# Loading order and step order in the head of a fused LayerNorm, state-space scan and gated-unit kernel

## The chip, the cores and the metric

The kernel runs on one core of a Trainium2 chip (trn2). The metric is the device time of one execution in microseconds (us). The kernel before was timed in three runs; their median is 185.26 us.

## The reference, cut to what matters

`x` has 2048 tokens of 448 features. Everything is computed from its normalised rows `xn`.

```python
xn = _layernorm(x)                        # 2048 x 448, no scale, no shift
s  = _A_ref(xn, Lambda_re, ..., Dskip)    # diagonal complex state-space scan over the tokens
g  = _silu(_B_ref(xn, w_gate, w_up, w_down))
return x + s * g

def _B_ref(x, w_gate, w_up, w_down):      # w_gate, w_up: 448 x 1792, w_down: 1792 x 448
    g = x @ w_gate
    u = x @ w_up
    return (_sigmoid(g) * u) @ w_down
```

## The kernel before, in words

The tokens are cut into 4 chunks (`c`) of 512, and each chunk into 4 tiles of 128 rows (`t` counts tiles from 0 to 15). A chunk needs the transposed rows `xnT`. It then passes through 14 steps that fill `hF` (7 "g" steps with `w_gate`, 7 "u" steps with `w_up`), a phase B (input matrix of the scan), the scan itself on VectorE, `down` (with `w_down`) and `yout` (output matrix of the scan, sum and store).

**A step.** The 448 features are contracted in 7 slices of 64 rows. `gu_mm` (lines 699 to 712) issues 7 pairs of matmuls per step: one of a pair (line 707) uses the lower 64 rows of TensorE and yields 128 columns of the first 896 of `w_gate` or `w_up`, the other (line 708) uses the upper 64 rows and yields 128 columns of the last 896. So the weight tiles `wG` and `wU` hold the lower half of the columns on partitions 0 to 63 and the upper half on 64 to 127, and step `m` of 7 needs its 128 columns of both halves. The two results fill the two banks of one of three PSUM slots, `gu[0]` to `gu[2]`, which the steps use in turn. `gu_evac` (lines 716 to 726) empties a slot: a g step by a tanh on ScalarE (line 721), a u step by one VectorE instruction (line 724). Two more banks, `acc[0]` and `acc[1]`, serve transposes, the phase B and the output.

**Order.** `Plan` (lines 74 to 242) records every operation with an engine, a planned cost and its dependences. It settles one order per engine from planned times, and the instructions are issued in that order. TensorE keeps the order in which the code adds its operations; VectorE does so too while `pl.seq` is true (lines 964 to 985); each DMA queue keeps the order of its loads. The `rate` of a load and its `slot` only enter the planned times. An engine works its list strictly in order, so an instruction that waits holds back all that follow it on its engine. The loads of SP and ACT share eight landing counters in turn: a load that reuses a counter is not issued before the earlier load on it has landed.

**The head, chunk 0.** For each of tiles 0 to 3: `stats` (VectorE, lines 424 and 425), `chain` (square root on ScalarE line 450, a copy of the mean on GpSimd line 451, reciprocal on VectorE line 452), `norm` (VectorE, line 469), `pe_transpose` (eight small TensorE instructions, lines 501 to 503, into `acc[0]` or `acc[1]`) and a copy to `xnT[0]` (tile 0 by ScalarE, line 506; the others by VectorE, line 509). TensorE first runs 11 warm-up matmuls on zeros (line 418). `columns` (lines 535 to 563) turns the three parameter rows `log_dt`, `Lambda_im`, `Lambda_re` (loaded by GpSimd's queue into `hF`) into columns with five small matmuls (lines 540 and 542) in `gu[2]`, copies them to `pv` by VectorE (line 546), and starts a chain of small GpSimd operations. From these ScalarE and VectorE make the tables of sines and cosines (`tables`, lines 570 to 605) that the scan needs.

TensorE's order in the head before is: warm-up; transposes of tiles 0 and 1; `columns`; g steps 0 and 1, each for tile 0 and then each for tile 1; transposes of tiles 2 and 3; g step 2 for tiles 0 and 1; g steps 0, 1, 2 for tiles 2 and 3 together; g steps 3 to 6 and u steps 0 to 6 for all four tiles; phase B.

The loads of the head before, in the order of their queues (sizes as the profile counts them):

- SP: x tile 0 (112 KB); lower half of w_gate for steps 0-1 (224 KB), 2-3 (224 KB) and 4-6 (336 KB); w_up steps 0-2, lower then upper half (336 KB each); x tiles 4 to 7 (448 KB); w_up steps 3-6, lower then upper half (448 KB each); D (`dbc`); then the transposing loads of B (`bT`, line 375) and the transposes of the normalised tiles 4 to 7.
- ACT: x tile 1 (112 KB); x tiles 2 and 3 (224 KB); upper half of w_gate for steps 0-1, 2-3 and 4-6.

Tiles 4 to 7 are the next chunk: `stats_for(1)` and `prepare(1)` normalise them (ScalarE, line 474), and DMA transposes write them to `xnT[1]`.

Of the kernel before, what the change touches and what calls it, by code (L numbers as in the profile page):

```python
# [14 lines left out]
ACT = mybir.ActivationFunctionType  # L15
# [5 lines left out]
P = 128  # L21
H = 64
# [4 lines left out]
TPC = L // P  # L27
# [35 lines left out]
def act(n, ap=0):  # L63
    return 0.05 + 0.000833 * n + 0.093 * ap
# [181 lines left out]
def kernel(  # L246
# [18 lines left out]
    V, A, G, T, Q = nc.vector, nc.scalar, nc.gpsimd, nc.tensor, nc.sync  # L265
# [80 lines left out]
    pl = Plan(185.0)  # L346
# [9 lines left out]
    def load_x(t0, n, q="SP", r=(), rate=230e3):  # L356
        load(q, [("x", t) for t in range(t0, t0 + n)], n * P * D * 2,
             x_all[:, t0:t0 + n, :], x_src[:, t0:t0 + n, :], r=r, rate=rate)

    BLK = {"g": [(0, 2), (2, 4), (4, 7)], "u": [(0, 3), (3, 7)]}  # L360

    def load_w(eng, k, half, b, r=(), rate=105e3):
        m0, m1 = BLK[k][b]
        ps = slice(half * H, half * H + H)
        c0 = half * 896
        load(eng, [("w", k, half, m) for m in range(m0, m1)], H * 7 * (m1 - m0) * P * 2,
             wgt[k][ps, :, m0 * P:m1 * P],
             wsrc[k][:, c0 + m0 * P:c0 + m1 * P].rearrange("(s p) f -> p s f", p=H), cost=0.65, r=r, rate=rate)

    def load_wd(h):  # L370
        fs = slice(h * 7, h * 7 + 7)
# [11 lines left out]
    def load_p(eng, k, r=()):  # L383
        load(eng, ("vrow", k), D * 2, vrow[k:k + 1, :], (A_log_dt, A_Lambda_im, A_Lambda_re)[k].unsqueeze(0), cost=0.75, r=r)
    load_x(0, 1, "SP")
    load_w("SP", "g", 0, 0, rate=90e3)
    load_w("SP", "g", 0, 1)
    load_x(1, 1, "ACT")
    load_x(2, 2, "ACT")
    load_w("ACT", "g", 1, 0, rate=90e3)  # L390
    load_w("SP", "g", 0, 2)
    load_w("ACT", "g", 1, 1)
    load_w("ACT", "g", 1, 2)
    load_p("POOL", 0)
    load_p("POOL", 1)
    load_p("POOL", 2)
# [7 lines left out]
    add("POOL", 0.1, lambda: G.memset(pio2[:], PI / 2), w=["pio2"])  # L404
    add("POOL", 0.6, lambda: G.iota(iota[:, 0:NTAB], pattern=[[1, NTAB]], base=0, channel_multiplier=0,
                                    allow_small_or_imprecise_dtypes=True), w=[("wv", 0)])
    for h in range(2):
        load_w("SP", "u", h, 0, rate=215e3)
    load_x(4, 4, rate=140e3)
    for h in range(2):  # L410
        load_w("SP", "u", h, 1, rate=260e3)
    load("SP", "dbc", P * D * 2, dbc[:], A_Dskip.unsqueeze(0).to_broadcast((P, D)))


# [6 lines left out]

    def stats(t):
        b = t % 3
        add("DVE", 0.6, lambda: V.bn_stats(out=bst[b][:], in_=x_all[:, t, :]), r=[("x", t)], w=[("bst", b)])  # L424
        add("DVE", 0.16, lambda: V.bn_aggr(out=mv[:, t, :], in_=bst[b][:]), r=[("bst", b)], w=[("mv", t)])

    def act_stats(t0):
# [67 lines left out]
    def pe_transpose(t):  # L495
        b, a, js = t % NXN, next_acc(), slice(t * P, t * P + P)
        tp = flat(acc[a][:].bitcast(BF16)[:, 0:7 * P], 7, P)

        def f():
            for s in range(6):  # L500
                T.transpose(tp[:, s, :], xn[b][:, s * H:s * H + P], ident[:, :])  # L501
            T.transpose(tp[0:H, 6, :], xn[b][:, 384:448], ident[:, :])
            T.transpose(tp[H:P, 6, :], xn[b][:, 0:H], ident[:, :])
        add("PE", 0.46, f, r=[("xn", b), "ident"], w=[("acc", a)])
        if t == 0:
            add("ACT", 0.85, lambda: A.copy(out=xnT[0][:, :, js], in_=tp[:, :, :]),
                r=[("acc", a)], w=[("xnT", 0, t, "a"), ("xnT", 0, t, "b")])
        else:
            add("DVE", 0.64, lambda: V.tensor_copy(out=xnT[0][:, :, js], in_=tp[:, :, :]),
                r=[("acc", a)], w=[("xnT", 0, t, "a"), ("xnT", 0, t, "b")])  # L510
# [9 lines left out]
    def xr(c, lo=0, hi=TPC):  # L520
        return [("xnT", c % 3, j, h) for j in range(lo, hi) for h in "ab"]
# [11 lines left out]


    def columns(a):
        vps = flat(gu[a][:, 0, 0:12], 4, 3)

        def f():
            for i in range(3):
                T.matmul(vps[:, i, :], lhsT=vrow[:, i * P:(i + 1) * P], rhs=ident[0:3, 0:3], start=True, stop=True)  # L540
            for h in range(2):
                T.matmul(vps[h * H:h * H + H, 3, :], lhsT=vrow[:, 384:448], rhs=ident[0:3, 0:3], start=True, stop=True)
        add("PE", 0.4, f, r=["ident"] + [("vrow", k) for k in range(3)], w=[("gu", a)])
        pv = sbt("pv", [3, 4], FP32)
        dt_b = C("dt", 4, BF16)
        add("DVE", 0.1, lambda: V.tensor_copy(out=pv[:].rearrange("p k i -> p i k"), in_=vps[:]), r=[("gu", a)], w=["pv"])
        dt_b = C("dt", 4, BF16)
        lim, lre = pv[:, 1, :], pv[:, 2, :]
        K.update(lre=lre, lim=lim)
        eb = expc[:].to_broadcast((P, 4))  # L550

        def small(fn, r, w):
            add("POOL", 0.4, fn, r=r, w=w)
        tt = lambda o, x, y, op: (lambda: G.tensor_tensor(out=o, in0=x, in1=y, op=op))
        theta, arg, turn, r_col = C("theta"), C("arg"), C("turn"), C("r")
# [9 lines left out]
    K = {}  # L565

    def silu_table():
        add("ACT", 1.3, lambda: A.preload_act_table_set("silu_and_others"), r=[("sd", t) for t in range(4)], w=["silutab"])

    def tables():  # L570
        turn = C("turn")
# [126 lines left out]

    def gu_mm(c, k, m, a, lo, hi, first):
        x = xnT[c % 3]  # L700
        ts = slice(lo * P, hi * P)
        w_ = wgt[k]
        ms = slice(m * P, m * P + P)

        def f():
            for s in range(7):
                T.matmul(gu[a][:, 0, ts], lhsT=w_[0:H, s, ms], rhs=x[0:H, s, ts], start=(s == 0), stop=(s == 6))  # L707
                T.matmul(gu[a][:, 1, ts], lhsT=w_[H:P, (s + 1) % 7, ms], rhs=x[H:P, s, ts],  # L708
                         start=(s == 0), stop=(s == 6))
        n = (hi - lo) * P  # L710
        return add("PE", 7 * (0.0028 + n / 2400.0) + (2 * SW if first else 0), f,
                   r=xr(c, lo, hi) + [("w", k, 0, m), ("w", k, 1, m)], w=[("gu", a)], name=f"{k}{c}.{m}")

    sg_n = [0]

    def gu_evac(c, k, m, a):
        b = m % NSIG
        th, tk = (hF[1][:, m, :, :], ("hF", 1, m)) if c == 0 else (sig[b][:], ("sig", b))
        ho, hk = hF[c % 2][:, m, :, :], ("hF", c % 2, m)
        if k == "g":  # L720
            add("ACT", act(1024), lambda: A.activation(th, gu[a][:], ACT.Tanh, scale=0.5),  # L721
                r=[("gu", a)], w=[tk])
        else:
            add("DVE", dve1(1024), lambda: V.scalar_tensor_tensor(out=ho, in0=th, scalar=1.0, in1=gu[a][:],  # L724
                                                                 op0=ALU.add, op1=ALU.mult),
                r=[("gu", a), tk], w=[hk])

    def gu_step(c, i, first=False):
        m, k = (i // 2, "gu"[i % 2]) if c else (i % 7, "gu"[i // 7])
# [237 lines left out]
    for t in (0, 1):  # L967
        chain(t, 1)
        norm(t)
    stats(2)  # L970
    stats(3)
    slots0 = [next_gu() for _ in range(3)]
    pe_transpose(0)
    pe_transpose(1)
    columns(slots0[2])
    for t in (2, 3):
        chain(t, 1)
        norm(t)
    for j in range(2):
        for m in range(2):  # L980
            gu_mm(0, "g", m, slots0[m], j, j + 1, not (j or m))
    pe_transpose(2)
    pe_transpose(3)
    silu_table()
    pl.seq = False
    gu_mm(0, "g", 2, slots0[2], 0, 2, True)
    for m in range(3):
        gu_mm(0, "g", m, slots0[m], 2, 4, False)
        gu_evac(0, "g", m, slots0[m])
    b_load()  # L990
    def stats_for(c):
        for t in range(4 * c, 4 * c + 4):
            if c not in (3,):
                stats(t)
            elif t % 2:
                act_stats(t - 1)
            if t % 2:
                chain(t - 1, 2)
# [96 lines left out]
```

## Time and profile before

| | |
|---|---|
| Time, three runs | 185.00, 185.26, 186.19 us; median 185.26 |
| Profiled execution, span on the core | 183.7 us |
| Lowest run minus span | 1.3 us |
| Median minus span | 1.6 us |
| TensorE busy | 177.4 us, 1402 matmuls |
| VectorE busy | 166.4 us, 296 instructions |
| ScalarE, GpSimd busy | 94.8 us, 34.2 us |
| Chain that ended last | TensorE 93%, DMA 3%, all else 4% |

The profile is of one execution. It gives its span from the first to the last instruction, and no device time of its own; what lies around the span is taken from the three runs. Times inside it count from the span's start. A line of the timeline has the start in us, the duration in us, the engine, the line of the code, the operation, what it writes and reads, and in brackets the time that the engine had stood idle with what ended the wait. "PEld" is the loading of weights into TensorE, and an engine with a "q" behind it is its instruction queue, where loads are issued.

### The profile page before, as it was taken

What the parts mean: (1) busy time and instruction counts of PE and PEld (TensorE: products, weight loads), DVE (VectorE), ACT (ScalarE), POOL (GpSimd) and SP (SyncE); (2) the same over time, 40 slices, a digit from 0 to 9 for tenths busy, and PEclk for the clock granted to TensorE, in tenths of its full rate; (3) what the DMA queues carried; (4) which work ended last, traced back from release to release, by engine and by line L of the source; (5) the groups of instructions that cost most, each with busy time, mean ns of one, the idle gap of its engine ahead of it and who ended that gap; (6) DMA issues with size and microseconds to landing.
All of it is one profiled execution on the core that took longest, in us unless ns stands there. A gap on an engine that the chain in (4) does not pass through costs nothing.

```text
span 183.7 us, 3601 instructions
## 1 busy us (share of the span) xinstructions
PE 177.4 (97%) x1402; PEld 90.4 (49%) x1402; DVE 166.4 (91%) x296; ACT 94.8 (52%) x152; POOL 34.2 (19%) x95
## 2 busy tenths in 40 slices
PE   7699999999999999999999999999999999999992
PEld 2585555465554444455554444444555444455551
DVE  3873899899999998999999999999999998999973
ACT  3689993958599978665310452367120445211100
POOL 7370465000048557700000000000000000000000
PEclk9999999999999999999999999999999999999999
DMA  5999994489801370243000000002000000001121
GB/s 137 255 225 223 155 166 90 90 256 266 231 0 26 74 82 21 50 82 71 0 2 0 29 0 0 4 0 75 0 4 0 25 25 5 25 0 52 57 73 50
DMA packets 30258, 13.44 MB, mean 73 GB/s; under 512 B 19744, under 2 KB 30240, under 8 KB 30240
## 3 DMA queue, kind: packets, MB, share of 16 engines
q1 hardware_dynamic: 28336, 12.05, 30.7%
q10 hardware_dynamic: 1808, 1.15, 2.5%
q8 instruction: 11, 0.18, 0.4%
q14 instruction: 7, 0.06, 0.1%
q0 software_dynamic: 96, 0.00, 0.0%
HBM read 6.77 MB, written 1.84 MB: 47 GB/s over the span
## 4 chain that ended last, share of the span: by engine, by line
PE 93%; DMA 3%; DVE 1%; issue 1%; POOL 1%; DVEq 0%; POOLq 0%
PE gu L707 45%; PE gu L903 14%; PE acc L932 11%; PE acc L903 9%; PE gu L775 8%; DMA hF<-in_A_Lambda_re_dram 3%; PE gu L708 2%; PE acc L778 2%; PE gu L761 2%; POOL hF L353 1%; PE acc L501 0%; DVE o_t L948 0%; PE acc L764 0%; DVE o_t L944 0%; DVE o_t L941 0%
## 5 line engine op out<-in xcount | busy, mean ns | idle before, releaser
L708 PE MATMUL gu<-xnT,wG 64*128 64x512 bf16 (+2 forms) x245 | 46.0, 333 | 0.0
L707 PE MATMUL gu<-xnT,wG 64*128 64x512 bf16 (+2 forms) x245 | 46.0, 333 | 0.0
L707 PE MATMUL gu<-xnT,wU 64*128 64x512 bf16 x196 | 45.8, 376 | 0.0
L708 PE MATMUL gu<-xnT,wU 64*128 64x512 bf16 x196 | 45.8, 376 | 0.0
L721 ACT ACTIVATE sig<-gu 128x1024 f32<-128x1024 f32 x21 | 21.3, 1021 | 22.0 <-PE gu L708 21.9
L903 PEld LDWEIGHTS <-hF 128*128 128x128 bf16 x224 | 21.9, 98 | 20.7 <-issue 0.2
L707 PEld LDWEIGHTS <-wG 64*128 64x128 bf16 x245 | 21.9, 94 | 18.7
L707 PEld LDWEIGHTS <-wU 64*128 64x128 bf16 x196 | 18.4, 94 | 22.1
L724 DVE SCALAR_TENSOR_TENSOR hF<-sig,gu 128x1024 bf16<-128x1024 f32 x21 | 25.5, 1216 | 2.9 <-PE gu L708 1.6
L903 PE MATMUL gu<-wd,hF 128*128 128x448 bf16 x140 | 27.9, 352 | 0.0
L842 DVE TENSOR_TENSOR_SCAN wv<-c_r,st,z 128x512 bf16<-128x512 f32 x18 | 22.9, 1276 | 0.0
L932 PE MATMUL acc<-cT,hT 128*128 128x448 bf16 (+1 forms) x112 | 22.6, 346 | 0.0
L708 PEld LDWEIGHTS <-wG 64*128 64x128 bf16 x245 | 21.8, 94 | 0.0
L909 ACT ACTIVATE g_t<-gu 128x448 bf16<-128x448 f32 x10 | 5.4, 541 | 29.2 <-DVE o_t L946 12.9
L708 PEld LDWEIGHTS <-wU 64*128 64x128 bf16 x196 | 18.4, 94 | 0.0
L789 ACT CAST bus<-gu 128x1024 bf16<-128x1024 f32 x12 | 11.9, 1011 | 12.4 <-PE gu L761 12.2
L903 PE MATMUL acc<-wd,hF 128*128 128x448 bf16 x84 | 16.9, 352 | 0.0
L775 PE MATMUL gu<-xnT,bT 128*128 128x512 bf16 x72 | 16.7, 379 | 0.0
L932 PEld LDWEIGHTS <-hT 128*128 128x128 bf16 x119 | 11.5, 98 | 10.1 <-issue 0.4
L424 DVE BATCH_NORM_STATS2 bst<-x_all 128x6 f32<-128x448 bf16 x12 | 7.0, 610 | 5.7 <-DMA x_all<-in_A_x_dram 5.7
L795 ACT CAST bus<-acc 64x256 bf16<-64x256 f32 (+1 forms) x24 | 8.8, 369 | 6.4 <-PE acc L778 6.1
L944 DVE TENSOR_TENSOR o_t<-acc,xd 128x448 bf16<-128x448 f32 (+1 forms) x16 | 9.6, 601 | 1.3 <-PE acc L932 1.2
(138 smaller groups left out, 240.1 us busy)
## 6 DMA issues: line engine op xcount, KB each, us to landing
out_dram<-o_t SPq DMA_DIRECT2D x15, 112.0 KB, 1.7
wd<-in_B_w_down_dram SPq DMA_DIRECT2D x2, 784.0 KB, 5.5
x_all<-in_A_x_dram SPq DMA_DIRECT2D x3, 448.0 KB, 4.5
wU<-in_B_w_up_dram SPq DMA_DIRECT2D x2, 448.0 KB, 12.2
wU<-in_B_w_up_dram SPq DMA_DIRECT2D x2, 336.0 KB, 7.6
wG<-in_B_w_gate_dram SPq DMA_DIRECT2D x2, 224.0 KB, 6.5
wG<-in_B_w_gate_dram ACTq DMA_DIRECT2D x2, 224.0 KB, 6.6
xnT<-xn SPq DMA_TRANSPOSE x24, 2.4
```

What stands on the lines that cost most here:

```text
L424: add("DVE", 0.6, lambda: V.bn_stats(out=bst[b][:], in_=x_all[:, t, :]), r=[("x", t)], w=[("bst", b)])
L707: T.matmul(gu[a][:, 0, ts], lhsT=w_[0:H, s, ms], rhs=x[0:H, s, ts], start=(s == 0), stop=(s == 6))
L708: T.matmul(gu[a][:, 1, ts], lhsT=w_[H:P, (s + 1) % 7, ms], rhs=x[H:P, s, ts], start=(s == 0), stop=(s == 6))
L721: add("ACT", act(1024), lambda: A.activation(th, gu[a][:], ACT.Tanh, scale=0.5), r=[("gu", a)], w=[tk])
L724: add("DVE", dve1(1024), lambda: V.scalar_tensor_tensor(out=ho, in0=th, scalar=1.0, in1=gu[a][:], op0=ALU.add, op1=ALU.mult), r=[("gu", a) ...
L775: T.matmul(gu[slots[pt]][:, i, :], lhsT=bT[:, kt, i, pt * P:pt * P + P], rhs=x[:, 2 * kt, :], start=(first and kt == 0), stop=(not first a ...
L789: add("ACT", act(1024), lambda: A.copy(out=bus[u][:], in_=gu[slots[pt]][:]), r=key(pt), w=[("bus", u)])
L795: add("ACT", 0.3, lambda ns=ns, d=d, q=q, l=l, i=i: A.copy(out=bus[u][d, l, ns], in_=acc[a3[i]][q, 0:256]), r=[("acc", a3[i])] + ([("bus", ...
L842: dve(1.194, lambda k=k: V.tensor_tensor_scan(out=wv[:, k, :], data0=rb, data1=z[:, k, :], initial=(st[pt][:, k, :] if c else 0.0), op0=AL ...
L903: T.matmul(d, lhsT=hF[c % 2][:, m, h, js], rhs=wd[:, ft, :], start=(ft == 0), stop=(ft == FT - 1))
L932: T.matmul(y, lhsT=hT[c % 2][:, hm, js], rhs=cT[:, cm, c0:c1], start=(i == 0 and not on_pe), stop=(i == 6))
L944: add("DVE", dve1(n), lambda od=od, y=y, c0=c0, c1=c1: V.tensor_tensor(out=od, in0=y, in1=xq[:, c0:c1], op=ALU.add), r=[key, ("xd", q)], w ...
```

## The change

The loads of the head are reordered so that all four x tiles of chunk 0 come first, two on each queue. Each block of w_gate is then loaded as a pair, lower half on SP and upper half on ACT, in blocks of 2, 2 and 3 steps. x tiles 4 to 7 go on SP right behind the second pair. w_up is no longer cut into steps: one load per half (784 KB), lower on SP, upper on ACT. The third upper block of w_gate and the upper half of w_up are issued by ScalarE's queue between its square roots: behind that of tile 1 and that of tile 2.

The resulting order of the queues, the landing counter that each issue waits for in brackets:

- SP: x0, x2, w_gate lower 0-1, lower 2-3, x4-7 (x0's), w_gate lower 4-6 (x2's), w_up lower (w_gate lower 0-1's), D (x3's), B re (w_gate lower 2-3's), ...
- ACT: x1, x3, w_gate upper 0-1, upper 2-3, two square roots, w_gate upper 4-6 (x1's), copy of tile 0 to `xnT`, square root of tile 2, w_up upper (w_gate upper 0-1's), square root of tile 3, copy of tile 2, table load, copy of `pv`, tanh of steps 0 to 2, ...

The order of the work changes with it. `columns` moves behind the transposes of tile 3, uses `acc[0]`, and its copy goes to ScalarE. The copy of tile 2 to `xnT` goes to ScalarE. `stats(4)` stands in VectorE's fixed order between the normalisation of tile 3 and the copy of tile 3. g step 2 is cut into tiles too, and g steps 0 to 2 run tile 2 and then tile 3 separately. g step 3 uses `acc[0]` and `acc[1]` in place of a `gu` slot, with two tanh instructions of half the size.

TensorE's order in the head after: warm-up; transposes of tiles 0 and 1; g steps 0 and 1, each for tiles 0 and 1; transposes of tile 2; g step 2 for tiles 0 and 1; transposes of tile 3; `columns`; g steps 0, 1, 2 for tile 2; g steps 0, 1, 2 for tile 3; g step 3 in the accumulators; g steps 4 to 6; u steps 0 to 6; phase B. It has 56 matmuls more (1458), all by the finer cuts.

On VectorE the copy of bT (line 651, needs the second transposing load of B re) now stands ahead of the evacuation of u step 0; before it stood behind three evacuations. On GpSimd and ScalarE the operations for the tables stand behind or between those of tiles 4 to 7.

```diff
-    BLK = {"g": [(0, 2), (2, 4), (4, 7)], "u": [(0, 3), (3, 7)]}
+    BLK = {"g": [(0, 2), (2, 4), (4, 7)], "u": [(0, 7)]}
...
     load_x(0, 1, "SP")
-    load_w("SP", "g", 0, 0, rate=90e3)
-    load_w("SP", "g", 0, 1)
     load_x(1, 1, "ACT")
-    load_x(2, 2, "ACT")
-    load_w("ACT", "g", 1, 0, rate=90e3)
-    load_w("SP", "g", 0, 2)
-    load_w("ACT", "g", 1, 1)
-    load_w("ACT", "g", 1, 2)
+    load_x(2, 1, "SP", rate=180e3)
+    load_x(3, 1, "ACT", rate=180e3)
+    load_w("SP", "g", 0, 0, rate=115e3)
+    load_w("ACT", "g", 1, 0, rate=115e3)
+    load_w("SP", "g", 0, 1, rate=165e3)
+    load_w("ACT", "g", 1, 1, rate=165e3)
+    load_x(4, 4, rate=230e3)
+    load_w("SP", "g", 0, 2, rate=150e3)
...
-    for h in range(2):
-        load_w("SP", "u", h, 0, rate=215e3)
-    load_x(4, 4, rate=140e3)
-    for h in range(2):
-        load_w("SP", "u", h, 1, rate=260e3)
+    load_w("SP", "u", 0, 0, rate=150e3, slot=10)
...
-        add("DVE", 0.6, lambda: V.bn_stats(out=bst[b][:], in_=x_all[:, t, :]), r=[("x", t)], w=[("bst", b)])
+        add("DVE", 0.6, lambda: V.bn_stats(out=bst[b][:], in_=x_all[:, t, :]),
+            r=[("x", t)] + ([("xnT", 0, 3, "a")] if 4 < t < 8 else []), w=[("bst", b)])
...
-        if t == 0:
+        if t in (0, 2):
...
-        vps = flat(gu[a][:, 0, 0:12], 4, 3)
+        vps = flat(acc[a][:, 0:12], 4, 3)
...
-        add("DVE", 0.1, lambda: V.tensor_copy(out=pv[:].rearrange("p k i -> p i k"), in_=vps[:]), r=[("gu", a)], w=["pv"])
+        add("ACT", 0.2, lambda: A.copy(out=pv[:].rearrange("p k i -> p i k"), in_=vps[:]), r=[("acc", a)], w=["pv"])
...
+        if a is None:
+            for i in range(2):
+                add("ACT", act(512), lambda i=i: A.activation(th[:, i, :], acc[i][:], ACT.Tanh, scale=0.5),
+                    r=[("acc", i)], w=[tk] if i == 0 else [(tk, 1)])
...
     for t in (0, 1):
         chain(t, 1)
         norm(t)
+    load_w("ACT", "g", 1, 2, rate=150e3, r=[("sd", 1)], slot=11)
     stats(2)
-    stats(3)
     slots0 = [next_gu() for _ in range(3)]
     pe_transpose(0)
     pe_transpose(1)
-    columns(slots0[2])
-    for t in (2, 3):
-        chain(t, 1)
-        norm(t)
-    for j in range(2):
-        for m in range(2):
+    chain(2, 1)
+    norm(2)
+    load_w("ACT", "u", 1, 0, rate=150e3, r=[("sd", 2)], slot=13)
+    stats(3)
+    chain(3, 1)
+    norm(3)
+    for m in range(2):
+        for j in range(2):
             gu_mm(0, "g", m, slots0[m], j, j + 1, not (j or m))
     pe_transpose(2)
+    stats(4)
+    for j in range(2):
+        gu_mm(0, "g", 2, slots0[2], j, j + 1, not j)
     pe_transpose(3)
+    columns(0)
     silu_table()
     pl.seq = False
-    gu_mm(0, "g", 2, slots0[2], 0, 2, True)
-    for m in range(3):
-        gu_mm(0, "g", m, slots0[m], 2, 4, False)
-        gu_evac(0, "g", m, slots0[m])
+    for j in range(2, 4):
+        for m in range(3):
+            gu_mm(0, "g", m, slots0[m], j, j + 1, False)
+            if j == 3:
+                gu_evac(0, "g", m, slots0[m])
+    gu_mm(0, "g", 3, None, 0, TPC, False)
+    gu_evac(0, "g", 3, None)
...
-    for i in range(3, 13):
+    for i in range(4, 13):
         gu_step(0, i)
```

More of the change, by code (lines that the diff above doesn't have):

```diff
@@ L358, in load_x, with load_w @@
              x_all[:, t0:t0 + n, :], x_src[:, t0:t0 + n, :], r=r, rate=rate)
-    BLK = {"g": [(0, 2), (2, 4), (4, 7)], "u": [(0, 3), (3, 7)]}
-    def load_w(eng, k, half, b, r=(), rate=105e3):
+    BLK = {"g": [(0, 2), (2, 4), (4, 7)], "u": [(0, 7)]}
+    def load_w(eng, k, half, b, r=(), rate=105e3, slot=None):
         m0, m1 = BLK[k][b]
@@ L368, in load_w @@
              wsrc[k][:, c0 + m0 * P:c0 + m1 * P].rearrange("(s p) f -> p s f", p=H), cost=0.65, r=r, rate=rate)
+        if slot is not None:
+            pl.ops[-1].slot = slot
     def load_wd(h):
@@ L542, in f @@
                 T.matmul(vps[h * H:h * H + H, 3, :], lhsT=vrow[:, 384:448], rhs=ident[0:3, 0:3], start=True, stop=True)
-        add("PE", 0.4, f, r=["ident"] + [("vrow", k) for k in range(3)], w=[("gu", a)])
+        add("PE", 0.4, f, r=["ident"] + [("vrow", k) for k in range(3)], w=[("acc", a)])
         pv = sbt("pv", [3, 4], FP32)
         dt_b = C("dt", 4, BF16)
-        add("DVE", 0.1, lambda: V.tensor_copy(out=pv[:].rearrange("p k i -> p i k"), in_=vps[:]), r=[("gu", a)], w=["pv"])
+        add("ACT", 0.2, lambda: A.copy(out=pv[:].rearrange("p k i -> p i k"), in_=vps[:]), r=[("acc", a)], w=["pv"])
         dt_b = C("dt", 4, BF16)
@@ L567, in silu_table @@
     def silu_table():
-        add("ACT", 1.3, lambda: A.preload_act_table_set("silu_and_others"), r=[("sd", t) for t in range(4)], w=["silutab"])
+        add("ACT", 1.3, lambda: A.preload_act_table_set("silu_and_others"), r=[("sd", t) for t in range(4)] + [("xnT", 0, 2, "a")], w=["silutab"])
     def tables():
@@ L700, in gu_mm @@
         x = xnT[c % 3]
+        bank, keys = ([gu[a][:, 0, :], gu[a][:, 1, :]], [("gu", a)]) if a is not None else (
+            [acc[0][:], acc[1][:]], [("acc", 0), ("acc", 1)])
         ts = slice(lo * P, hi * P)
@@ L706, in f @@
             for s in range(7):
-                T.matmul(gu[a][:, 0, ts], lhsT=w_[0:H, s, ms], rhs=x[0:H, s, ts], start=(s == 0), stop=(s == 6))
-                T.matmul(gu[a][:, 1, ts], lhsT=w_[H:P, (s + 1) % 7, ms], rhs=x[H:P, s, ts],
+                T.matmul(bank[0][:, ts], lhsT=w_[0:H, s, ms], rhs=x[0:H, s, ts], start=(s == 0), stop=(s == 6))
+                T.matmul(bank[1][:, ts], lhsT=w_[H:P, (s + 1) % 7, ms], rhs=x[H:P, s, ts],
                          start=(s == 0), stop=(s == 6))
@@ L711, in gu_mm @@
         return add("PE", 7 * (0.0028 + n / 2400.0) + (2 * SW if first else 0), f,
-                   r=xr(c, lo, hi) + [("w", k, 0, m), ("w", k, 1, m)], w=[("gu", a)], name=f"{k}{c}.{m}")
+                   r=xr(c, lo, hi) + [("w", k, 0, m), ("w", k, 1, m)], w=keys, name=f"{k}{c}.{m}")
     sg_n = [0]
@@ L719, in gu_evac @@
         ho, hk = hF[c % 2][:, m, :, :], ("hF", c % 2, m)
-        if k == "g":
+        if a is None:
+            for i in range(2):
+                add("ACT", act(512), lambda i=i: A.activation(th[:, i, :], acc[i][:], ACT.Tanh, scale=0.5),
+                    r=[("acc", i)], w=[tk] if i == 0 else [(tk, 1)])
+        elif k == "g":
             add("ACT", act(1024), lambda: A.activation(th, gu[a][:], ACT.Tanh, scale=0.5),
@@ L725, in gu_evac @@
                                                                  op0=ALU.add, op1=ALU.mult),
-                r=[("gu", a), tk], w=[hk])
+                r=[("gu", a), tk] + ([(tk, 1)] if (tk, 1) in pl.w else []), w=[hk])
     def gu_step(c, i, first=False):
@@ L993, in stats_for @@
             if c not in (3,):
-                stats(t)
+                if t != 4:
+                    stats(t)
             elif t % 2:
```

## The prediction

> **What bounds the kernel now.** I read the page's busy times first, then the engines' busy time by stretch, TensorE's timeline of the head, and last the loads. The page:
>
> ```profile
> PE 177.4 (97%) x1402; PEld 90.4 (49%) x1402; DVE 166.4 (91%) x296; ACT 94.8 (52%) x152; POOL 34.2 (19%) x95
> ```
>
> Stretches (start:end, length, busy time of PE, PEld, DVE, ACT, POOL):
>
> ```profile
> 5.00:8.00 3.00, 1.67 (x25) 1.26 (x27) 2.67 (x8) 1.77 (x5) 0.37 (x2) 1.00 1.08 260
> 8.00:20.00 12.00, 12.00 (x186) 8.61 (x184) 7.12 (x18) 10.93 (x15) 4.67 (x12) 1.00 1.20 225
> 20.00:36.00 16.00, 16.00 (x132) 8.11 (x130) 15.20 (x33) 12.69 (x26) 7.48 (x30) 1.00 0.76 115
> 36.00:100.00 64.00, 64.00 (x483) 32.28 (x480) 62.42 (x101) 42.00 (x72) 18.23 (x34) 1.00 0.37 85
> 100.00:179.00 79.00, 79.00 (x569) 38.05 (x568) 75.55 (x129) 25.37 (x35) 0.00 (x0) 1.00 0.06 22
> ```
>
> TensorE never pauses from 8 to 179 us. So the time moves with the moment at which TensorE gets through the head, and any new gap is paid in full. Its marks there:
>
> ```profile
> 6.40 0.24 PE L503 MATMUL acc<-ident,xn 128*64 128x128 bf16 x1
> 7.63 0.21 PE L540 MATMUL gu<-ident,hF 3*128 3x3 bf16 x3 [0.99 <-DMA hF<-in_A_Lambda_re_dram]
> 7.89 0.23 PE L707 MATMUL gu<-xnT,wG 64*128 64x128 bf16 x1
> ...
> 9.56 0.51 PE L501 MATMUL acc<-ident,xn 128*128 128x128 bf16 x6
> ...
> 10.79 0.28 PE L707 MATMUL gu<-xnT,wG 64*128 64x256 bf16 x1
> ...
> 13.87 0.38 PE L707 MATMUL gu<-xnT,wG 64*128 64x512 bf16 x1
> ...
> 19.91 0.38 PE L707 MATMUL gu<-xnT,wU 64*128 64x512 bf16 x1
> ```
>
> The reader sees one wait (0.99 us, for parameter rows), g step 3 from 13.87 and u step 0 from 19.91: 6.04 for four whole steps, 1.51 each. What the change lets TensorE wait for is loads. Bytes and rate in four stretches: 4.5 to 6.5 us (both queues load halves of weights), 6.5 to 11 (the same, blocks of unequal size), 12 to 19 (SP alone, mostly one half at a time), 39 to 42 (w_down, all 128 partitions):
>
> ```profile
> DMA packets 1160, 0.55 MB, mean 276 GB/s; under 512 B 86, under 2 KB 1160, under 8 KB 1160
> DMA packets 1587, 1.07 MB, mean 237 GB/s; under 512 B 56, under 2 KB 1587, under 8 KB 1587
> DMA packets 1723, 1.55 MB, mean 222 GB/s; under 512 B 59, under 2 KB 1722, under 8 KB 1722
> DMA packets 1282, 1.13 MB, mean 378 GB/s; under 512 B 16, under 2 KB 1282, under 8 KB 1282
> ```
>
> The last figure of an issue is the time from issue to landing (issues at 3.1, 8.41, 9.76 and 13.29 us):
>
> ```profile
> wG<-in_B_w_gate_dram ACTq DMA_DIRECT2D x1, 336.0 KB, 9.1
> ...
> x_all<-in_A_x_dram SPq DMA_DIRECT2D x1, 448.0 KB, 10.6
> ...
> wU<-in_B_w_up_dram SPq DMA_DIRECT2D x1, 448.0 KB, 12.7
> ...
> bT<-in_A_B_re_dram SPq DMA_TRANSPOSE x1, 12.1
> ```
>
> They landed at 12.2, 19.0, 22.4 and 25.4. VectorE waited 3.69 us for x tiles 4 to 7 without harm, since only chunk 1 needs them; the change puts such a wait on the path.
>
> **The change part by part.**
>
> *First weights, and columns moved.* Before, the first block landed at 7.1 (SP, 336 KB up to its end on that queue) and 7.6 (ACT, 560 KB). After, both queues have 448 KB up to it; the sum is the same, so both halves should land near the middle, 7.35 (bounds 7.1 and 7.6). Tile 0 is copied at 6.98, so g step 0 starts at 7.35 in place of 7.89, because the 0.26 of columns and its wait are gone from there. The x tiles now ahead cost nothing that the rows show.
>
> *TensorE's list up to the end of steps 0 to 2.* A step takes 0.39 per tile (28 matmuls of 128 columns, 7.89 to 9.45), 0.77 for two tiles: cutting is nearly free, and each switch between kinds of matmul takes about 0.1. A transpose of a tile takes 0.62, columns 0.26. After: 7.35, four tile pieces 1.66, transposes of tile 2 0.62 (to 9.63), g step 2 0.88, transposes of tile 3 0.62, columns 0.26 (to 11.4), three pieces for tile 2 1.17, three for tile 3 1.17: 13.75 if nothing waits, against 13.87. So the best gain is about 0.1, or 0.5 if the weights came by 7.0. The second block (1344 KB in all; 1267 KB had landed by 9.06 and 1472 by 9.84) lands near 9.35, ahead of its use at 9.63.
>
> *The new wait.* stats(4) needs x tiles 4 to 7 and stands ahead of the copy of tile 3 on VectorE. That load has 1120 KB up to its end on SP, with ACT equally busy. Nearest row: ACT's third block, also with 1120 KB up to its end, landed at 12.2. SP's rows (896 KB at 11.1, 1232 KB at 14.2) interpolate to 13.2; the 448 KB alone at 378 GB/s behind 9.35 give 10.6. I take 12.2, the row with the same bytes. Then stats and aggregate take 0.76, the copy 0.59, handovers 0.1: tile 3 is ready at 13.65, where TensorE wants it at 12.58. Queued behind it on VectorE are the stats of tiles 5 to 7; on TensorE, everything. Steps 0 to 2 end at 13.65 + 1.17 = 14.82, which is 0.95 later than 13.87.
>
> *Third w_gate block.* Used at 14.82 + 1.51 = 16.33. SP has 1456 KB up to it: 672 KB of both queues after 12.2, at 237 GB/s 2.9 us, 15.1. Covered by 1.2; by the old curve (1568 KB on SP at 15.9) it would still be covered.
>
> *w_up in halves.* u step 0 now needs both whole loads, and is wanted at 14.82 + 6.04 = 20.86. After 12.2 there remain 1792 KB (1.84 MB): at 276 GB/s 18.9, at 237 19.9, and if the same bytes take as long as before, 22.4. I take 19.9, the row with both halves in flight. Covered by 1.0; beyond that each us costs one.
>
> *Issues on ACT.* Two more, about 0.64 each. The w_gate issue stands before the copy of tile 0, which waits for transposes until 6.07 anyway; square root 1 ends at 5.06. The w_up issue waits until 7.35 and ends near 8.0; behind it stands square root 3, whose input comes near 8.6. Nothing.
>
> *VectorE's bT copy ahead of u step 0.* The first B load landed 3.0 after the last of w_up (25.4 against 22.4). Behind 19.9 that gives 22.9; copy 0.3, one product 0.3, evacuation 1.2: slot free at 24.7, wanted by u step 3 at 20.86 + 4.54 = 25.4. Covered by 0.7.
>
> *Tables later, step 3 in accumulators.* Parameter columns reach GpSimd at 12.1, not 8.2. ScalarE's run of tables, tanh and normalisation took 10.04 to 28.82, 18.8, and then it stood 3.19 idle. Started at 14.05, with 0.1 for the split tanh, it ends at 32.95; phase B wants it at 32.01 + 0.95 = 32.96. If late, 0.9 more is hidden (a slot emptied at 35.88 was used at 36.79).
>
> Sum: +0.95. The profile's span of 183.7 becomes 184.65; the median lies 1.6 above the span, so 185.26 + 0.95 = **186.2**.
>
> [...] The paired load of halves is slower in the rows (237 and 276 GB/s) than a full-width one (378); one half at a time made 222. [...]
>
> **The rivals.**
>
> *No new wait.* Tiles 4 to 7 land by 11.1 and the rest in time: only the list counts, −0.1, down to −0.5: 185.0. For it: 378 GB/s at full width. Against: 222 to 276 with halves in flight.
>
> *w_up is late (slower side).* Pairing brings no rate, and the same 4032 KB land at 22.4. u step 0 starts at 22.4 against 19.91, +2.5; B at 25.4 frees the slot at 27.3 where 26.9 is wanted, +0.35: 188.1. It decides from a landing after 20.86. For it: SP's loads issued from 8.41 on took 10.6 to 12.7 to land; against: SP then ran alone.
>
> *VectorE is held by bT.* w_up in time, but B lands at 25.4 as before: slot free at 27.2, 1.8 behind 25.4, on top of 0.95: 188.0. For it: SP issues the transposes one by one; against: its queue holds 2352 KB before them in place of 3024.
>
> **How the numbers follow.** Forecast 0.50 (its own range 185.5 to 187.2, from 11.5 to 13.2 for tiles 4 to 7), no wait 0.22, late w_up 0.17, bT 0.11. The range 184.7 to 188.2 takes in −0.5 and both slow rivals. 1%, about what a measurement tells from no change, is 1.85. Faster by that needs more than the 0.99 wait and the whole of columns: 0.02. Slower (over 187.1): most of the slow rivals and the forecast's upper end, 0.28. Within: 0.70.
>
> **What would show it.** Right: TensorE idle about 1.1 us before the pieces for tile 3, with stats(4) on VectorE starting near 12.2; first w_gate matmul near 7.35; u step 0 near 20.9 without a wait. Wrong: tiles 4 to 7 before 11; a wait for wU; a wait of u step 3 on VectorE; a gap after phase B on ScalarE.

## The result and the profile after

The changed kernel takes 190.75 us (median of four runs, 189.89 to 192.19), against 185.26 before: 1.028 times, interval 1.0208 to 1.0352. The prediction was 186.2, range 184.7 to 188.2: it missed, and on the slow side. The profiled execution took 190.5 us; its span is 188.7, 5.0 over the kernel before. Executions of one kernel here spread over 0.8 to 4.9 us, in part because a stretch of half clock (below) comes in some and not in others (granted clock over the span 0.989 to 1.0 in the four of the changed kernel), so a trace tells of its own execution and a median of all.

The page of the changed kernel, busy time and the clock that TensorE was granted in 40 slices of 4.7 us:

```profile
PE 180.1 (95%) x1458; PEld 90.0 (48%) x1458; DVE 166.5 (88%) x294; ACT 95.7 (51%) x155; POOL 36.1 (19%) x95
...
PEclk9999799999999999999999999999999999999999
```

The same stretches as before, TensorE first, the clock third from the end:

```profile
5.00:8.00 3.00, 2.23 (x50) 1.91 (x52) 2.67 (x9) 1.20 (x3) 0.20 (x2) 1.00 1.16 278
8.00:20.00 12.00, 9.86 (x192) 6.64 (x188) 7.61 (x22) 7.39 (x10) 5.82 (x15) 0.92 1.13 254
20.00:36.00 16.00, 16.00 (x143) 7.30 (x138) 12.15 (x19) 14.42 (x27) 6.70 (x28) 0.95 0.69 103
36.00:50.00 14.00, 13.13 (x117) 7.32 (x116) 11.84 (x20) 10.51 (x18) 0.00 (x0) 1.00 0.93 237
```

From 8 to 50 us TensorE, which never paused before, is idle for 3.0 us and has a clock under 1. Its longest waits (line, what it waited for, sum, times, longest):

```profile
PE acc L710 <- issue: 2.1, 1, 2.1
PE gu L417 <- DVE hF L380: 1.2, 1, 1.2
PE acc L909 <- ACT bus L801: 0.9, 1, 0.9
```

The second of them is at the start and was there before; the others are new. The first in the timeline, with the end of steps 0 to 2 ahead of it:

```profile
13.60 0.22 PE L710 MATMUL gu<-xnT,wG 64*128 64x128 bf16 x1
13.63 0.38 PE L709 MATMUL acc<-xnT,wG 64*128 64x512 bf16 x1
...
14.28 0.38 PE L709 MATMUL acc<-xnT,wG 64*128 64x512 bf16 x1
16.80 0.39 PE L710 MATMUL acc<-xnT,wG 64*128 64x512 bf16 x1 [2.14 <-issue]
...
20.25 0.63 PE L710 MATMUL gu<-xnT,wG 64*128 64x512 bf16 x1
20.68 0.63 PE L710 MATMUL gu<-xnT,wG 64*128 64x512 bf16 x1
...
23.68 0.38 PE L709 MATMUL gu<-xnT,wU 64*128 64x512 bf16 x1
```

The reader sees three things. Steps 0 to 2 end at 13.63, which is 0.24 sooner than before (13.87): the head itself does what the change is for. Then TensorE stops in the middle of g step 3, between the two matmuls of its fourth pair, which have the same tiles, weights and banks as the pairs ahead; the profile names no engine and no load, only "issue". And from 18.08 to 21.50 the clock is at half, a matmul pitch (from the start of one pair to that of the next) of 0.427 in place of 0.216. So the 5.0 us are: −0.24 for the head, 2.3 for the stop (14.28 to 16.80, less a pitch), 1.7 for 3.4 us of half clock, 1.03 for a pause at 48.2, and 0.2 left over.

What was running between 14.1 and 15.4 us on the DMA engines:

```profile
DMA packets 263, 0.49 MB, mean 374 GB/s; under 512 B 0, under 2 KB 262, under 8 KB 262
## 3 DMA queue, kind: packets, MB, share of 16 engines
q10 hardware_dynamic: 133, 0.24, 50.6%
q1 hardware_dynamic: 129, 0.23, 48.5%
q8 instruction: 1, 0.02, 5.4%
```

The last line is a load of 16 KB of instructions (queue 8 has 11 loads, 0.18 MB in all, in this trace). It starts at 14.18 and ends at 15.29, and it is the first on its queue; TensorE goes on 1.5 us behind its end. In the kernel before, the first one ran from 14.99 to 16.38, and TensorE worked through it. That gives the theory for the experiments.

### The profile page after: what moved, and what is told of

Read it like the earlier page. It is cut to its first block, busy times and chain, and to the rows that moved or that the text cites. A ratio compares the mean times of both kernels' runs of the same rounds, so it can differ in the third digit from the quotient of the medians.

```text
span 188.7 us, 3714 instructions
## 1 busy us (share of the span) xinstructions
PE 180.1 (95%) x1458; PEld 90.0 (48%) x1458; DVE 166.5 (88%) x294; ACT 95.7 (51%) x155; POOL 36.1 (19%) x95
## 4 chain that ended last, share of the span: by engine, by line
PE 86%; DVE 6%; issue 3%; ACT 2%; DMA 1%; DVEq 0%
PE gu L709 33%; PE gu L909 14%; PE acc L938 11%; PE gu L710 10%; PE acc L909 9%; PE gu L781 5%; PE gu L767 1%; DMA x_all<-in_A_x_dram 1%; PE acc L784 1%; ACT bus L801 1%; DVE z L844 1%; DVE wv L848 1%; PE acc L501 1%; DVE ta L841 1%; DVE tb L842 1%
## 5 line engine op out<-in xcount | busy, mean ns | idle before, releaser
L709 PE MATMUL gu<-xnT,wG 64*128 64x512 bf16 (+2 forms) x266 | 46.7, 322 | 0.4 <-ACT xnT L506 0.4
L710 PE MATMUL gu<-xnT,wG 64*128 64x512 bf16 (+2 forms) x266 | 46.7, 322 | 0.0
L709 PE MATMUL gu<-xnT,wU 64*128 64x512 bf16 x196 | 45.8, 376 | 0.0
L710 PE MATMUL gu<-xnT,wU 64*128 64x512 bf16 x196 | 45.8, 376 | 0.0
L709 PEld LDWEIGHTS <-wG 64*128 64x128 bf16 x273 | 22.8, 96 | 16.3
L709 PEld LDWEIGHTS <-wU 64*128 64x128 bf16 x196 | 18.4, 94 | 17.1
L710 PEld LDWEIGHTS <-wG 64*128 64x128 bf16 x273 | 22.7, 96 | 7.0 <-issue 4.8
L795 ACT CAST bus<-gu 128x1024 bf16<-128x1024 f32 x12 | 11.9, 1009 | 12.3 <-PE gu L767 12.2
L938 PEld LDWEIGHTS <-hT 128*128 128x128 bf16 x119 | 11.5, 98 | 10.1 <-issue 0.4
L781 PEld LDWEIGHTS <-bT 128*128 128x128 bf16 x72 | 7.0, 98 | 7.5
```

Source lines behind the costliest of these rows:

```text
L709: T.matmul(bank[0][:, ts], lhsT=w_[0:H, s, ms], rhs=x[0:H, s, ts], start=(s == 0), stop=(s == 6))
L710: T.matmul(bank[1][:, ts], lhsT=w_[H:P, (s + 1) % 7, ms], rhs=x[H:P, s, ts], start=(s == 0), stop=(s == 6))
L781: T.matmul(gu[slots[pt]][:, i, :], lhsT=bT[:, kt, i, pt * P:pt * P + P], rhs=x[:, 2 * kt, :], start=(first and kt == 0), stop=(not first a ...
L795: add("ACT", act(1024), lambda: A.copy(out=bus[u][:], in_=gu[slots[pt]][:]), r=key(pt), w=[("bus", u)])
L938: T.matmul(y, lhsT=hT[c % 2][:, hm, js], rhs=cT[:, cm, c0:c1], start=(i == 0 and not on_pe), stop=(i == 6))
```

## The experiments

**Theory "supply".** TensorE has run out of instructions. The cuts put 112 more (56 matmuls, each with its weight load) ahead of this point, and the first transfer comes only 0.8 us sooner. **Rivals:** "weights" (the third block of w_gate is late) and "accumulators" (step 3 in `acc`).

**Runs 1 to 4: the number of instructions.** (Runs are counted in the order in which they are told.) In the kernel before, warm-up matmuls in eighths; in the kernel before, the cuts alone; in the changed kernel, the cuts taken back; and then the warm-up in eighths too.

```diff
-    warm_mm(9)
+    warm_mm(72, 64)
```
```diff
-    gu_mm(0, "g", 2, slots0[2], 0, 2, True)
-    for m in range(3):
-        gu_mm(0, "g", m, slots0[m], 2, 4, False)
-        gu_evac(0, "g", m, slots0[m])
+    for j in range(2):
+        gu_mm(0, "g", 2, slots0[2], j, j + 1, not j)
+    for j in range(2, 4):
+        for m in range(3):
+            gu_mm(0, "g", m, slots0[m], j, j + 1, False)
+            if j == 3:
+                gu_evac(0, "g", m, slots0[m])
```

> The kernel before with one edit: the 9 warm-up matmuls of 512 columns are issued as 72 of 64 columns (same columns, same engine time, 126 TensorE instructions more, counting weight loads). Loads, order and all else are as before. Theory 'supply' (TensorE has no instructions left at about its 447th, until the first instruction transfer on queue 8 has come, at 15 to 16.4 us in the kernel before): the 447th instruction is now what was the 321st, reached at about 13.9 us; TensorE stops there, within a step and with all weights in place, until 16 to 17, and some half clock may follow: 187.2 to 190. Theory 'weights' (the stop of the changed kernel is a late third w_gate block) and theory 'accumulators' (it comes from step 3 in acc): neither is touched here, no stop, 185.3 within 0.3.

> The kernel before with only the finer cuts of the change: g step 2 in two tile pieces for tiles 0 and 1, and g steps 0 to 2 for tile 2 and then tile 3; 112 TensorE instructions more, loads and all else as before. Theory 'supply': the 447th instruction is reached near 14.3 us; TensorE stops there until about 16.5 (+2.2), and if the half clock follows from the stop, +1.7 more: 187.4 to 189.4. Theories 'weights' and 'accumulators': +0.3 at most for the cuts themselves, 185.3 to 185.8.

> The changed kernel with the cuts taken back: g step 2 for tiles 0 and 1 in one, g steps 0 to 2 for tiles 2 and 3 together; 112 TensorE instructions fewer; loads, step 3 in the accumulators and the rest as in the change. Theory 'supply': no stop inside g step 3 and no half clock at 18 us; in their place TensorE waits about 1.1 us for tile 3 (copied at 12.4, three double pieces behind it: end of steps 0 to 2 near 14.8); 186.2, or 187.2 if the wait of 1.0 after the first phase B stays. Theory 'weights': step 4 and the third block are as in the change, the stop stays until 16.8: 189 to 191. Theory 'accumulators': the same, 189 to 191.

> The kernel of the run with the cuts taken back, with the warm-up matmuls as 72 of 64 columns: the 126 instructions are put back at a place where no tile, load or accumulator is concerned. Theory 'supply': the stop comes back, near 13.5 to 15 us at about the 447th instruction, until 16 to 17: 1.5 to 4.5 slower than the kernel without them. Theories 'weights' and 'accumulators': equal to it within 0.3.

Measured, with the kernel before at 185.69: 186.24 (ratio 1.0032), 187.79, 190.66 (1.0253) and 192.65 (1.036). The cuts alone (second run) bring the stop to the kernel before, with its loads and slots; TensorE's timeline of that run:

```profile
14.78 0.38 PE L707 MATMUL gu<-xnT,wG 64*128 64x512 bf16 x1
16.67 0.39 PE L708 MATMUL gu<-xnT,wG 64*128 64x512 bf16 x1 [1.52 <-issue]
```

Half clock follows from 17.08 to 20.49. Three of its nine executions have such a stretch (this one, and 189.7 and 189.9), the others took 186.2 to 188.3, 1.0069 times the kernel before (1.0025 to 1.0112): the stop and the half clock are two losses. So "weights" and "accumulators" are out. The first run missed: 126 instructions more in the warm-up make no stop. The fourth is 2.0 slower than the third, as "supply" had it, but its trace (190.59, its fastest execution) has no such stop either, so that forecast came in for another reason, which stays open. The transfer is not at a fixed time: it came at 10.38 and 11.76 there, while TensorE needed it at 13.5 and 17.1. The reading that fits is that it is asked for by the count, and that more instructions early on ask for it earlier; the last run below tests it. The third run missed the other way: no stop in g step 3, yet no time gained. Its waits from 8 to 20 us, and those of TensorE in the whole run:

```profile
...
DVE bst L423 <- DMA x_all<-in_A_x_dram: 1.6, 1, 1.6
PE gu L709 <- DVE xnT L509: 1.5, 1, 1.5
```
```profile
PE acc L909 <- ACT bus L801: 2.0, 1, 2.0
PE gu L709 <- DVE xnT L509: 1.5, 1, 1.5
```

Here is the wait that the prediction forecast (statistics of tile 4 in front of the copy of tile 3). In the changed kernel the cuts cover it, because the three pieces for tile 2 run meanwhile. And a wait of 2.0 at 48 us. Each has a half clock behind it in this execution (192.68; granted clock 0.86 from 8 to 20 us and 0.91 from 50 to 70); the other three, without, took 189.7 to 191.3, and what held them no trace shows.

**Runs 5 to 8: one repair at a time.** The copies for C behind the emptying of the second phase B; g step 2 joined; cuts, statistics and C copies repaired at once; the same with `columns` early.

```diff
     pl.solve({"g0.0": 5.5})
+    ev = max(o.start for o in pl.ops if o.name == "evac1")
+    for n, o in enumerate(sorted((pl.ops[i] for i in c_ops), key=lambda o: (o.start, o.idx))):
+        o.start = max(o.start, ev + 0.001 * (n + 1))
```
```diff
-    for j in range(2):
-        gu_mm(0, "g", 2, slots0[2], j, j + 1, not j)
+    gu_mm(0, "g", 2, slots0[2], 0, 2, True)
```

> The changed kernel with ScalarE's copies for the scaled C matrix (line 673, which wait for the transposing load of C) put behind the copies that empty the accumulators of the second phase B, as the kernel before has them; nothing ahead of 40 us differs. Theory 'order' (the pause of TensorE at 48 us comes from that place in ScalarE's list): the 1.0 us pause goes, the stop at 14 us and the half clock stay: 189.7. Rival 'C is late for another reason' (the pause comes with the load, wherever the copies stand): 190.7.

> The changed kernel with only g step 2 for tiles 0 and 1 joined again: 28 TensorE instructions fewer ahead of g step 3. Theory 'supply' (TensorE stops at its 441st to 447th instruction unless the first instruction transfer has come 1.4 us before): the 447th is reached 14 matmul pitches of 0.108 later, near 15.7 instead of 14.2, the transfer is asked for at the same place and comes as before (14.2 plus 1.1), so a stop of 1.0 or less is left at the same instruction, in g step 4, too short for a half clock: about 187.6, or 189.3 if the half clock comes all the same. A rival, that the stop belongs to a time (the loads of 14 to 17 us) and not to an instruction: stop still from 14.3, 190.5.

> The changed kernel with its three pauses taken away as I read them: cuts taken back (no stop of supply), the statistics of tile 4 behind the copy of tile 3 (no wait for tiles 4 to 7), transposes of tile 3 straight behind those of tile 2 with g step 2 between them and the pieces (as before), and the copies for C behind phase B. Parameter columns late as in the change, step 3 in the accumulators, loads as in the change. If these three and the half clocks that follow them are the whole loss: steps 0 to 2 end at 13.4 (13.87 before), 184.8 to 185.3, so 0 to 0.5 under the kernel before. Rival 'tables' (parameter columns late make ScalarE late for phase B): a pause of up to 2 at phase B, 186 to 187.

> As the kernel of the run with the three pauses taken away, but with the parameter columns behind g step 0 for tiles 0 and 1, in acc[0], so that the tables start about 3 us sooner. Theory 'supply': equal to it within 0.3 if ScalarE is not late for phase B there. Rival 'tables': 1 to 2 faster than it.

Measured, with the kernel before at 185.31: 191.42 (1.0311), 192.04 (1.0361), 193.88 and 192.33 (1.033). The first three missed. Run 8 is 1.5 under run 7 in the medians, but their executions overlap (190.6 to 194.1 against 190.5 to 195.4), so this pair does not tell whether late columns cost anything. In run 6 the stop shrank as the count said, and yet:

```profile
PE acc L909 <- ACT bus L801: 3.0, 1, 3.0
PE gu L417 <- DVE hF L380: 1.2, 1, 1.2
PE gu L710 <- issue: 0.5, 1, 0.5
```

TensorE arrived sooner at 45.8 and waited there until 49.2, with half clock behind it (granted clock 0.97 from 36 to 50 us, 0.94 from 50 to 70). In run 8, with no stop at all, it waits at 60.6 (run 7 waits 4.1 there):

```profile
PE gu L709 <- ACT bus L795: 2.1, 1, 2.1
PE gu L417 <- DVE hF L380: 1.2, 1, 1.2
PE gu L767 <- DVE hF L730: 0.7, 1, 0.7
```

So something else stands right behind the stop. ScalarE's timeline of the changed kernel shows it (L801 empties the accumulators that TensorE's line 909 wants, L673 are the copies for C):

```profile
44.75 0.67 ACT L673 ACTIVATE ctmp<-xnT,c_n2i 128x448 f32<-128x448 bf16 x1 [0.34 <-DMA xnT<-in_A_C_im_dram]
45.32 0.66 ACT L673 ACTIVATE ctmp<-xnT,c_n2r 128x448 f32<-128x448 bf16 x1
45.88 0.35 ACT L801 CAST bus<-acc 128x256 bf16<-128x256 f32 x1
47.98 0.67 ACT L673 ACTIVATE ctmp<-xnT,c_n2i 128x448 f32<-128x448 bf16 x1 [1.75 <-DVE cT L676]
48.67 0.75 ACT L801 CAST bus<-acc 64x256 bf16<-64x256 f32 x2
```

In the kernel before all of those casts stand together, ahead of the copies:

```profile
41.76 1.91 ACT L795 CAST bus<-acc 128x256 bf16<-128x256 f32 x5 [1.30 <-PE acc L778]
43.69 1.01 ACT L789 CAST bus<-gu 128x1024 bf16<-128x1024 f32 x1
...
47.77 0.66 ACT L673 ACTIVATE ctmp<-xnT,c_n2i 128x448 f32<-128x448 bf16 x1
```

The diff touches none of these lines. The planner does. It plans the queues ahead of C as done sooner (half of w_up has left SP), so it puts the first copy for C at 41.5 of its own times, not 47.3, and with it the scaling on VectorE and the statistics of tiles 8 to 11, ahead of the rest of chunk 0's scan. The second phase B it plans at 40.0 and 40.2. My repair in run 5 moved the copies, but the statistics then stood ahead on VectorE and waited 4.3 us for their load, and the pause went to 61.8. **Theory "order"**: this order from about 36 us on is a second cause, of its own. **Rival "slack"**: VectorE, 91% busy before, has lost time in the head, and that returns in any order.

**Runs 9 to 12: order against head.** In these and the next four runs each transposing load is two plain loads of the same bytes; the transposition is left out, so they are compared with each other:

```diff
-        add("SP", 1.2, lambda: Q.dma_start_transpose(out=o, in_=i), r=r, w=keys, dma=nbytes * 1.5, chain=chain)
+        add("SP", 1.2, lambda: [Q.dma_start(out=o[h * H:h * H + H], in_=i[h * H:h * H + H]) for h in range(2)],
+            r=r, w=keys, dma=nbytes * 1.5, chain=chain)
```

and in the second pair a table `LATER` of the other kernel's planned times sets the order of what that planner puts at 36 us or later:

```diff
+    seen = {}
+    for o in reversed(pl.ops):
+        k = o.eng + "|" + getattr(o.fn, "__qualname__", "none").split(".<locals>.", 1)[-1].replace(".<locals>", "")
+        n = seen[k] = seen.get(k, -1) + 1
+        if n < len(LATER.get(k, ())) and LATER[k][n] is not None:
+            o.start = 1000.0 + LATER[k][n]
     with tc.manual_schedule():
         pl.emit()
```

> A base for the three runs sent with it. The kernel before, with each transposing load replaced by two plain loads of the same bytes into the same tile, one per half of the partitions (so B, C and the normalised rows of chunks 1 to 3 are used as they lie: the transposition is left out, all other work is done, in the planner's own order, which does not change). SP's stretch for a load stays near 1.2 us, the loads of C may land 1 to 3 sooner. 184 to 186 by every theory.

> The changed kernel with the same replacement (transposition left out). Theory 'supply' and theory 'order' alike: the stop at 14 us within g step 3 and its half clock stay (+4 on the plain kernel before, less 0.24). By 'order' the pause behind the second phase B is between 0 and 3, by when C lands: if C lands before 43, none. 188 to 191; if it is within 1 of the plain kernel before, the losses were tied to the transposing loads.

> The plain kernel before (transposition left out) up to the planner's 36 us, and from there the order in which the changed kernel's planner puts the operations (scaling of C and the statistics of tiles 8 to 11 some 6 us sooner, ahead of the rest of chunk 0's scan). No stop at 14 us, no change in the head. Theory 'order': ScalarE and VectorE come to those operations at 41 to 44 us and wait for the loads of C and x, TensorE then waits behind the second phase B or at 60 for the emptying of its last bank: 2 to 5 slower than the plain kernel before. Rival 'slack' (VectorE's time lost in the head is what counts): equal to it within 0.5.

> The plain changed kernel (transposition left out) with the order of the kernel before from its planned 36 us on. The stop at 14 us and its half clock stay. Theory 'order': no pause behind 36 us, so 3.5 to 4 over the plain kernel before, and 0 to 3 under the plain changed kernel. Rival 'slack': no faster than the plain changed kernel, with a pause at another place.

Measured, with the ratio to the kernel before (185.5): 185.75 (1.0022, 0.9976 to 1.0069), 190.14 (1.0233, 1.0166 to 1.0299), 190.36 (1.0228, 1.0151 to 1.0306) and 189.32 (1.0188, 1.0127 to 1.025). All four lie where "order" had them. The plain kernels stand to each other much as the originals do (4.4 apart, 5.5 there). The head of before with the order of after loses 4.6 us, which puts "slack" out. The stop alone, with the order of before, costs 3.6; that it is 0.8 under the plain changed kernel is not clear of the noise, but its trace has no pause behind the stop. The waits of the third from 36 to 60 us:

```profile
...
ACT ctmp L704 <- DMA xnT<-in_A_C_im_dram: 4.9, 1, 4.9
PE acc L934 <- ACT bus L826: 3.6, 1, 3.6
```

ScalarE stands 4.9 us in front of C, and TensorE 3.6 for the cast queued behind. Then half clock, in that run's stretches:

```profile
44.00:48.50 4.50, 0.86 (x5) 0.30 (x4) 2.08 (x4) 2.86 (x7) 0.00 (x0) 1.00 0.79 238
48.50:54.00 5.50, 5.50 (x21) 2.47 (x21) 5.22 (x13) 5.45 (x9) 3.32 (x6) 0.69 0.01 3
```

**Runs 13 to 16: both taken back, and the count once more.**

> Both causes taken back at once: the plain changed kernel (transposition left out), g step 2 for tiles 0 and 1 joined (28 TensorE instructions fewer ahead of the stop; with the transposing loads 0.5 of the stop was left and no half clock), and the order of the kernel before from its planned 36 us on. Theory 'two causes' (instruction supply with its half clock, and the planner's order; each hides behind the other): 1.3 over the plain kernel before, 184.7 of span, 186.5 to 187.3; that is 3 under the plain changed kernel. Rival 'a third thing': 189 or more.

> The changed loads and step 3 in the accumulators, with all cuts taken back, columns behind g step 0, statistics of tile 4 behind the copy of tile 3, and the order of the kernel before from its planned 36 us on (transposition left out). Theory 'two causes': no stop of supply, no half clock; u steps 1.1 late on VectorE before the first phase B as in the run with the transposing loads: 186 to 186.9; 185.5 if the plain load of B removes that wait. Rival 'a third thing': 189 or more.

> As the run before it, but with the parameter columns late, where the change puts them. Theory 'two causes' holds nothing against late columns except that ScalarE's tables end near 33 there, so 1 to 2.5 slower than that run: 187 to 189. If it is equal within 0.4, late columns cost nothing.

> The plain changed kernel with the order of before (stop at 14.5 until 16.9), with the warm-up as 72 matmuls of 64 columns: 126 TensorE instructions more ahead. Theory 'supply' (the first transfer is asked for at about the 185th instruction, comes 3 to 5 us later in this stretch, and is needed by the 447th): the transfer is asked for near 7.2 instead of 9.4 and comes at 10.4 to 11.8; the 447th instruction is the old 321st, reached at 12.3: so the stop is near 12.3, in the pieces for tiles 2 and 3, and ends by 13.0 to 14.4; the second transfer is needed 256 later, in g step 5 near 20, and is there. 1 to 3 faster than 189.3. Rival 'a time, not an instruction' (the loads of 14 to 17 us): the stop stays at 14.5 to 16.9.

Measured, with the kernel before at 185.34: 186.5 (1.0054, 1.0006 to 1.0102), 188.29 (1.0135, 1.0089 to 1.0181), 187.18 (1.0105, 1.0071 to 1.0139) and 188.73 (1.0194, 1.0161 to 1.0227). With both causes taken back by the two smallest edits, 3.6 of the plain changed kernel's 4.4 are gone. TensorE's waits there:

```profile
PE gu L449 <- DVE hF L412: 1.2, 1, 1.2
PE gu L742 <- issue: 0.3, 1, 0.3
PE gu L741 <- DMA wG<-in_B_w_gate_dram: 0.3, 1, 0.3
```

Run 14 missed by 1.4 and run 15 was not slower than it: late columns cost nothing to be seen. What is left in these two is small waits of TensorE: for w_gate's first block, ahead of g step 0 (0.8 in run 14, 0.6 in run 15), for w_up, ahead of u step 0 (0.9 and 0.3), and for VectorE (1.1 and 0.3). Without a stop, the loads are what TensorE meets next. In run 14 the matmul's line names ScalarE's normalisation of a later tile, which it does not use; the weight load just ahead of it waited 1.39 for w_up:

```profile
21.34 0.39 PE L741 MATMUL gu<-xnT,wU 64*128 64x512 bf16 x1 [0.90 <-ACT xn L506]
21.34 0.09 PEld L741 LDWEIGHTS <-wU 64*128 64x128 bf16 x1 [1.39 <-DMA wU<-in_B_w_up_dram]
```

Run 16 is the sharpest test of the count, for where its stop should stand was worked out ahead. The stop moved 2.1 us forward against run 12, into the pieces for tile 2 (12.3 said):

```profile
12.43 0.22 PE L742 MATMUL gu<-xnT,wG 64*128 64x128 bf16 x1
13.72 0.23 PE L741 MATMUL gu<-xnT,wG 64*128 64x128 bf16 x1 [1.08 <-issue]
```

Its time did not follow as forecast: 188.73 is 0.6 under run 12, not 1 to 3. TensorE's records (matmuls and weight loads, the two counts in the rows) up to the end of the stop, in the changed kernel and here:

```profile
0.00:16.79 16.79, 12.71 (x223) 8.56 (x223) 9.71 (x31) 9.37 (x14) 7.62 (x28) 1.00 0.94 239
0.00:13.71 13.71, 10.95 (x223) 9.44 (x223) 8.64 (x25) 5.65 (x9) 5.16 (x22) 1.00 0.89 223
```

446 records stand ahead of the stop, whatever they are, in all eight kernels that have one: the changed kernel, runs 2, 5 and 6, and runs 10, 12, 13 and 16. In each, TensorE goes on 1.3 to 1.7 us behind the end of the first transfer. In the ten other kernels with a trace, the transfer had ended 1.9 us or more before the 447th record.

No version here beats the kernel before.

## Why the prediction was wrong

*Right.* The first block of weights was in time: g step 0 started at 7.07 (7.35 said, bounds 7.1 to 7.6; in runs 13 to 15, with the same loads up to there, 7.20 to 7.86). TensorE's list ended at 13.63 (13.75 said), begun 0.28 sooner. w_up landed at 18.3 and 19.6 (19.9 said). ScalarE was not late for the first phase B (idle 1.05 ahead of it), and holds up nothing in run 15 either.

*Right by luck.* No wait for w_up, and none for VectorE in the u steps: TensorE was 3.8 late by then. Where the stop is gone, both rivals show themselves: w_up is waited for in runs 14 and 15, and in run 7 VectorE idles 1.62 for B, and TensorE then 1.10 for VectorE at u step 3.

*Wrong in size: the new wait.* Tiles 4 to 7 landed at 11.06, not 12.2, and the copy of tile 3 was done at 12.41, when TensorE wanted it: the +0.95 was 0. No faster rate did this: from 9 to 11 us all queues moved 200 GB/s, under the 237 of the row. The term that was wrong is "with ACT equally busy": from 8 to 10.5 us SP's queue moved 0.53 MB and ACT's 0.04 (why ACT's third block, issued by 5.4, started so late is not shown). Later the paired halves of w_up ran at 374 GB/s (14.1 to 15.4; 327 from 14 to 18), near the full-width row of 378, so 19.9, worked out at 237 throughout, came near by rates that were off both ways. The 11.5 at which the forecast's own range begins is shown by no run: here they landed at 11.06. The mechanism itself was real: VectorE did wait 1.34 for the load, and run 3, without the cuts, pays 1.5 us for it.

*The step that failed first: "cutting is nearly free".* It was priced by durations (0.39 per tile, 0.77 for two). The price was in the count: 112 instructions more ahead of the first transfer, a stop of 2.3 and 1.7 of half clock. The trace of before held the sign: its first transfer of instructions came as late, at 14.99, with TensorE at its 346th record.

*The step that was missing: the order behind the head.* The prediction followed ScalarE and VectorE only to the first phase B. The planner's times changed with the loads, and with them the order from 36 us on, which alone costs the kernel before, in its plain form, 4.6.

*The sum.* Alone, in the plain kernels, the stop costs 3.6 and the order 4.6; together they cost 4.4 there (5.5 in the originals), not 8.2. The traces fit this: a TensorE that is 3.8 late at 45 us waits 1.0 for C in place of 3.6 with a half clock behind it. So each repair alone gave little or nothing.

## What to carry to other kernels

Count the instructions of an engine up to each transfer of its instructions, and not only their time, before cutting matmuls finer: here the cut was free until the count reached a block that had not come (446 records ahead of a stop of 2.1 us). Where a planner sets the order, compare the whole order of both kernels, behind the edit too, and ask of each moved instruction what load it waits for. When a repair of the wait that you see gives nothing, look for the wait that stood behind it, and take both away in one run.

## What the runs showed of the hardware

*Supply of instructions.* The transfers are of 16 KB, and further on in the changed kernel they start at TensorE's records 1198, 1438, 1689 and 1950, some 250 apart (240, 251 and 261, where the expectation of run 16 has 256). Counted back (an inference) the first is due near record 185, at 9.4 us; it started 4.8 us later, with the DMA engines busy (share 1.13 from 8 to 20 us), and 3.0 later in run 1. That the load on the DMA engines is what held it was not tested. In the loaded head here the transfer was not hidden: TensorE stood for 2.1 us in the changed kernel, 1.5 in run 2 and 1.1 in run 16.

*The clock.* Half clock came in pieces of 3.4 us (18.08 to 21.50 in the changed kernel, 17.08 to 20.49 in run 2), 1.3 and 0.4 us behind the end of an idle time of TensorE (2.14 until 16.80 and 1.52 until 16.67). How long it had stood is no sharp rule: in run 5 a stop of 1.8 us was followed by none (granted clock 1.00 from 8 to 36 us), and so was an idle time of 1.6 us in run 4 (47.94 to 49.53; granted clock 1.00 from 36 to 100). What sets it is not shown.
